# Moving every store from GpSimd's software ring to SyncE's ring, beside the loads

## The chip, the cores and the metric

The kernel runs on one core of one Trainium2 chip. The metric is device time in microseconds (us), taken over several executions; the profile is one execution, and its span is about 2 us shorter than the reported time. All timed runs below that are compared with one another were in the fast state. The four copy kernels were run once each, so their state is unknown, and only single stretches of their traces are used.

## The reference

The forward pass mixes two branches with a scalar gate: attention of one query over a cache (32 heads, 4096 keys, head size 128) and a small MLP with the mish activation. The kernel returns the output and nine gradients.

```python
def _fwd_reference(A_x, A_k_cache, A_v_cache, A_wq, A_wo, B_x, B_w1, B_b1, B_w2, gate_w):
    # ... (_A_ref: q = x @ wq; p = softmax(q k^T / sqrt(128)); o = p v; return o @ wo)
    # ... (_B_ref: h = x @ w1 + b1; return (h * tanh(softplus(h))) @ w2)
    x = A_x
    g = _sigmoid((x * gate_w).sum(-1, keepdims=True))
    a = _A_ref(x, A_k_cache, A_v_cache, A_wq, A_wo)
    b = _B_ref(x, B_w1, B_b1, B_w2)
    return g * a + (1 - g) * b

def reference(A_x, A_k_cache, ..., grad_out):     # arguments cut
    _out, _vjp = jax.vjp(_f, A_x, A_k_cache, A_v_cache, A_wq, A_wo, B_w1, B_b1, B_w2, gate_w)
    return (jnp.asarray(_out), *[jnp.asarray(_g) for _g in _vjp(grad_out)])
```

What matters for the time: K and V are 32 MB each, and so are their gradients dK and dV. With the weights and their gradients 82 MB are read and 82 MB written, all in bfloat16.

## The kernel before

Each head is one period. The loads of K and V (1 MB each) are issued three heads ahead by SyncE into four buffers each; dK of the head before is stored early in a period, dV of this head late, both by GpSimd, from a pool of five buffers. The transfers of one issuer stand in line in its ring: the page lists SyncE's as q1 (hardware) and GpSimd's as q0 (software). Sixteen DMA engines carry each transfer in packets, and each engine leaves a landing mark when its part is done. The tile of `wo` is overwritten in place by its gradient, stored, and its buffer loaded anew.

```python
    def load_k(h):
        if h < H:
            kts[h] = kv_in.tile([P, J, Dh], BF16, name="Kn", tag="Kn", bufs=KB)
            nc.sync.dma_start(kts[h][:], Kv[h])
    # ... (load_v, load_wq, load_w2 and w1 are alike)
    def load_wo(g):
        if g < NG:
            wos[g] = wts.tile([P, G, D], BF16, name="wo_g", tag="wo_g", bufs=3)
            nc.sync.dma_start(wos[g][:], wo_v[g])
    # ...
    def dk_half(h, half):
        # ... (VectorE: outer product of ds and q, one half of the 4096 rows)
        if h == H - 1:
            a, b = half * (J // 2), (half + 1) * (J // 2)
            nc.gpsimd.dma_start(dKv[h][:, a:b, :], st["dK"][:, a:b, :])
        elif half == 1:
            nc.gpsimd.dma_start(dKv[h], st["dK"][:])
    # ... (dv_half is alike)
    for h in range(H):
        hh, g = h % G, h // G
        if hh == 3:
            load_wo(g + 2)
            # ... (load_wq every second group)
        load_k(h + 3)
        load_v(h + 3)
        # ...
        period(h)     # holds dk_half(h - 1, 0..1) early and dv_half(h, 0..1) late
    # ... (last gradients, then the small outputs)
    nc.gpsimd.dma_start(dwq_v[:, :, CL:], dwq_l[:])
```

## Time and profile before

| | before |
|---|---|
| time, median of 4 runs | 417.73 us (417.38 to 418.01) |
| span of the profile | 415.7 us |
| last store (dwq_l) landed: first / fifteenth / last of its sixteen marks | 403.2 / 404.2 / 411.4 us |
| from the last landing to the end of the span | 4.3 us |

The prediction below shows and reads the page's rows. Three further views are needed for the comparison. First the DMA issues of the page (last column: median us from issue to landing):

```profile
Kn<-in_A_k_cache_dram SPq DMA_DIRECT2D x32, 1024.0 KB, 27.0
Vn<-in_A_v_cache_dram SPq DMA_DIRECT2D x32, 1024.0 KB, 27.8
out_dram<-dV_sb POOLq DMA_DIRECT2D x32, 1024.0 KB, 12.3
out_dram<-dK_sb POOLq DMA_DIRECT2D x31, 1024.0 KB, 12.4
```

Then the wait for an output buffer, from the costliest groups (count, then busy us and mean ns of one, then idle time before and what ended it):

```profile
L557 DVE TENSOR_TENSOR dV_sb<-p_bf,qd 128x2048 bf16<-128x2048 bf16 x64 | 78.0, 1218 | 4.1 <-DMA out_dram<-dK_sb 4.1
```

Last, the closing drain of GpSimd (the instructions of the program's last line; durations in ns, min/median/max, then the first and last start in us):

```profile
L788 POOLq DRAIN  x3: 45/102/17856, 397.0 to 415.4; - x3
```

The longest of these three drains starts at 397.05 us, right behind GpSimd's last issue, and lasts 17.856 us, to 414.9. The last store had landed at 411.4. So for 3.5 us no data moves and the program waits for GpSimd alone. The prediction passed this by: it took the time after the last landing as fixed.

### The profile page before, as it was taken

The page shows a single profiled execution, that of the slowest core. Times are in us where ns is not written, and L with a number is a line of the kernel's source. Part 1 is how long each engine was busy: PE and PEld are TensorE (multiplying, and loading weights), DVE is VectorE, ACT ScalarE, POOL GpSimd, SP SyncE. Part 2 cuts the span into 40 slices and gives each one's busy share as a digit, 9 for nine tenths or more (in the row PEclk, how much of TensorE's full clock was granted, in tenths as well). Part 3 has the DMA queues.
Part 4 walks back from the last instruction along what each step waited for, and adds up shares of the span by engine and source line. Part 5 has one row for each costly group of instructions (what it writes and reads, how often), then busy time and mean ns, then how long its engine had stood idle before and what let it go on. Part 6 is the DMA issues. An engine that isn't in the chain of part 4 may idle for free.

```text
span 415.7 us, 15639 instructions
## 1 busy us (share of the span) xinstructions
PE 305.6 (74%) x6932; PEld 281.1 (68%) x6932; DVE 308.2 (74%) x804; ACT 174.4 (42%) x394; POOL 49.3 (12%) x92
## 2 busy tenths in 40 slices
PE   0787999888998788788877688429888788876200
PEld 0676888888987677787767687428777678876200
DVE  2348666665679999989897688528999997967850
ACT  1354444334445455354533346305553545553000
POOL 0001110111110111121111112001111111132310
PEclk9999999969999999989996899958999999998655
DMA  8999999999999999999999999999999999998980
GB/s 280 419 401 335 420 424 417 420 423 423 421 423 420 420 404 415 424 420 423 423 410 426 423 414 411 419 422 381 405 411 423 419 419 422 421 422 351 401 314 14
DMA packets 26336, 165.06 MB, mean 397 GB/s; under 512 B 2812, under 2 KB 2812, under 8 KB 10012
## 3 DMA queue, kind: packets, MB, share of 16 engines
q1 hardware_dynamic: 14116, 82.03, 48.6%
q0 software_dynamic: 12112, 82.03, 47.7%
q8 instruction: 54, 0.88, 0.8%
q14 instruction: 14, 0.11, 0.1%
q10 hardware_dynamic: 40, 0.01, 0.0%
HBM read 82.03 MB, written 82.03 MB: 395 GB/s over the span
## 4 chain that ended last, share of the span: by engine, by line
DMA 37%; DVE 30%; PE 21%; ACT 6%; issue 2%; ACTq 0%; DVEq 0%
DMA Kn<-in_A_k_cache_dram 30%; PE tr L535 7%; DVE dK_sb L557 7%; DVE dV_sb L557 6%; DMA out_dram<-dK_sb 6%; ACT tT L537 5%; DVE junk L354 4%; PE sA L601 3%; PE sA L543 3%; PE sB L654 3%; DVE junk L268 3%; PE h_ps L385 2%; DVE junk L486 2%; DMA vec_rows<-in_gate_w_dram 1%; DVE wo_g L343 1%
## 5 line engine op out<-in xcount | busy, mean ns | idle before, releaser
L537 ACT COPY tT<-tr 128x512 f32<-128x512 f32 x256 | 142.9, 587 | 153.1 <-PE tr L535 153.0
L543 PEld LDWEIGHTS <-tT 128*128 128x128 bf16 x2048 | 75.8, 98 | 37.0 <-ACT tT L537 31.6
L535 PE MATMUL tr<-ident_bf,Kn 128*128 128x128 bf16 x1024 | 79.2, 230 | 9.4 <-DMA Kn<-in_A_k_cache_dram 8.2
L557 DVE TENSOR_TENSOR dV_sb<-p_bf,qd 128x2048 bf16<-128x2048 bf16 x64 | 78.0, 1218 | 4.1 <-DMA out_dram<-dK_sb 4.1
L557 DVE TENSOR_TENSOR dK_sb<-ds_bf,qd 128x2048 bf16<-128x2048 bf16 x64 | 77.7, 1216 | 0.0
L535 PEld LDWEIGHTS <-Kn 128*128 128x128 bf16 x1024 | 66.2, 104 | 10.9 <-DMA Kn<-in_A_k_cache_dram 9.3
L535 PE MATMUL tr<-ident_bf,Vn 128*128 128x128 bf16 x1024 | 72.8, 221 | 0.2 <-DMA Vn<-in_A_v_cache_dram 0.2
L543 PE MATMUL sA<-qdc,tT 128*128 128x48 bf16 x1024 | 49.2, 188 | 23.0 <-ACT dq_all L659 16.3
L535 PEld LDWEIGHTS <-Vn 128*128 128x128 bf16 x1024 | 63.2, 100 | 1.4 <-issue 0.7
L543 PE MATMUL sB<-qdc,tT 128*128 128x48 bf16 x1024 | 46.3, 183 | 0.6 <-issue 0.6
L654 PE MATMUL sB<-ds_bf,Kn 128*128 128x48 bf16 x1024 | 32.6, 185 | 7.7 <-DVE ds_bf L643 4.8
L584 POOL DMA_DIRECT2D out_dram<-dV_sb x32 | 18.3, 571 | 169.1 <-DVE dV_sb L557 82.1
L601 PEld LDWEIGHTS <-Vn 128*128 128x128 bf16 x1024 | 30.3, 96 | 10.4 <-issue 10.3
L601 PE MATMUL sA<-e_bf,Vn 128*128 128x48 bf16 x1024 | 30.9, 183 | 7.4 <-DVE zs L621 5.4
L574 POOL DMA_DIRECT2D out_dram<-dK_sb x31 | 17.7, 570 | 153.1 <-DVE rz L623 84.6
L654 PEld LDWEIGHTS <-Kn 128*128 128x128 bf16 x1024 | 29.7, 97 | 8.3 <-issue 8.3
L605 DVE TENSOR_REDUCE m<-sA 128x1 f32<-128x32 f32 x32 | 6.1, 189 | 31.7 <-PE sA L543 31.5
L268 DVE SCALAR_TENSOR_TENSOR junk<-wo_g,da_bc 128x640 bf16<-128x640 bf16 x32 | 26.3, 821 | 2.9 <-DMA wo_g<-in_A_wo_dram 1.2
L354 DVE SCALAR_TENSOR_TENSOR junk<-wq_g,dq_bc 128x1024 bf16<-128x1024 bf16 (+1 forms) x25 | 25.1, 1004 | 0.2
L385 PE MATMUL h_ps<-cols_bf,w_sb 128*96 128x1 bf16 x90 | 18.3, 314 | 1.2 <-ACT qd L279 0.5
L641 DVE TENSOR_SCALAR_CACHE_REDUCE dj<-sB,rz 128x128 f32<-128x128 f32 x32 | 11.1, 345 | 10.8 <-PE sB L635 10.8
L385 PEld LDWEIGHTS <-w_sb 128*96 128x96 bf16 x90 | 17.6, 272 | 1.6 <-issue 0.6
(137 smaller groups left out, 277.5 us busy)
## 6 DMA issues: line engine op xcount, KB each, us to landing
Kn<-in_A_k_cache_dram SPq DMA_DIRECT2D x32, 1024.0 KB, 27.0
Vn<-in_A_v_cache_dram SPq DMA_DIRECT2D x32, 1024.0 KB, 27.8
out_dram<-dV_sb POOLq DMA_DIRECT2D x32, 1024.0 KB, 12.3
out_dram<-dK_sb POOLq DMA_DIRECT2D x31, 1024.0 KB, 12.4
wq_g<-in_A_wq_dram SPq DMA_DIRECT2D x4, 1280.0 KB, 21.8
wo_g<-in_A_wo_dram SPq DMA_DIRECT2D x8, 640.0 KB, 13.3
out_dram<-wo_g POOLq DMA_DIRECT2D x8, 640.0 KB, 11.3
out_dram<-dwq_t POOLq DMA_DIRECT2D x5, 896.0 KB, 16.2
```

What stands on the lines that cost most here:

```text
L268: nc.vector.scalar_tensor_tensor(junk[:, 0:D], in0=wos[g][:, i, :], scalar=1.0, in1=da_bc[:], op0=ALU.mult, op1=ALU.mult, accum_out=gp["do ...
L354: nc.vector.scalar_tensor_tensor(junk[:, c0:c1], in0=wqs[w][:, rc, c0:c1], scalar=1.0, in1=dq_bc[:, w * WG * Dh + c0:w * WG * Dh + c1], op ...
L385: nc.tensor.matmul(hps[a][:, fc:fc + 1], lhsT=w1_sb[:, rc, :].rearrange("p (q c) -> p q c", c=FCN)[:, :, fc], rhs=x_bf[:, rc:rc + 1], star ...
L535: nc.tensor.transpose(tp[:, t, :], src[:, c * 8 + t, :], ident_bf[:])
L537: nc.scalar.copy(f32v(sb[:].rearrange("p a b -> p (a b)")), f32v(tp[:].rearrange("p a b -> p (a b)")))
L543: nc.tensor.matmul(out[:, j:j + W], lhsT=tb[:, t, :], rhs=vec.to_broadcast([P, W]), start=True, stop=True)
L557: nc.vector.tensor_tensor(dst[:, a:b, :].rearrange("p j (a b) -> p j a b", b=2), col[:, a:b, :].unsqueeze(2).to_broadcast([P, n, Dh // 2, 2]),
L574: nc.gpsimd.dma_start(dKv[h], st["dK"][:])
L584: nc.gpsimd.dma_start(dVv[h], st["dV"][:])
L601: nc.tensor.matmul(O, lhsT=vts[h][:, j, :], rhs=st["e"][:, j:j + 1].to_broadcast([P, W]), start=(j == 0), stop=(j == J - 1))
L641: nc.vector.tensor_scalar(dj[:], PT, rz[:], None, ALU.mult, ALU.add, accum_out=dd[:])
L654: nc.tensor.matmul(DQ, lhsT=kts[h][:, j, :], rhs=ds[:, j, 0:1].to_broadcast([P, W]), start=(j == 0), stop=(j == J - 1))
```

## The change

All stores that GpSimd issued are issued by SyncE, in the order in which the program states them, so they stand on the same hardware ring as the loads (one small output stays on ScalarE, as before). The intent is to have one ring in the program's own order, no software ring, and a GpSimd with nothing to do. Nothing else changes; the instructions of TensorE, VectorE and ScalarE are the same.

```diff
-            nc.gpsimd.dma_start(dwo_v[g], wos[g][:])
+            nc.sync.dma_start(dwo_v[g], wos[g][:])
 ...
-            nc.gpsimd.dma_start(dKv[h], st["dK"][:])
+            nc.sync.dma_start(dKv[h], st["dK"][:])
 ...
-            nc.gpsimd.dma_start(dVv[h], st["dV"][:])
+            nc.sync.dma_start(dVv[h], st["dV"][:])
 ...
-    nc.gpsimd.dma_start(dwq_v[:, :, CL:], dwq_l[:])
+    nc.sync.dma_start(dwq_v[:, :, CL:], dwq_l[:])
 ... (the same for dw2, db1, dw1, the two halves of the last dK, and dwq)
```

> **What bounds the kernel now.** I read the row of DMA tenths first, then the queue table, then single stretches of time, then the waits of SyncE's queue, and last the marks that each transfer leaves when it lands.
>
> The page of the kernel before:
>
> ```profile
> span 415.7 us, 15639 instructions
> ...
> PE 305.6 (74%) x6932; PEld 281.1 (68%) x6932; DVE 308.2 (74%) x804; ACT 174.4 (42%) x394; POOL 49.3 (12%) x92
> ...
> DMA  8999999999999999999999999999999999998980
> GB/s 280 419 401 335 420 424 417 420 423 423 421 423 420 420 404 415 424 420 423 423 410 426 423 414 411 419 422 381 405 411 423 419 419 422 421 422 351 401 314 14
> ...
> q1 hardware_dynamic: 14116, 82.03, 48.6%
> q0 software_dynamic: 12112, 82.03, 47.7%
> q8 instruction: 54, 0.88, 0.8%
> ```
>
> No compute engine is above 74%, while the DMA digits are 9 nearly everywhere and the rate sits at 420 GB/s. The two big queues hold 48.6% + 47.7% = 96.3% of the time of 16 engines: q1 is the loads (SyncE), q0 the stores (GpSimd). So this is a copy of 82 MB in and 82 MB out with arithmetic beside it.
>
> The same in stretches (columns: window, length, busy time per engine, granted clock, DMA share, GB/s):
>
> ```profile
> 12.00:22.00 10.00, 6.49 (x96) 5.64 (x94) 3.48 (x12) 3.51 (x8) 0.00 (x0) 1.00 1.01 416
> 40.00:140.00 100.00, 88.37 (x1853) 83.16 (x1853) 67.26 (x180) 44.30 (x102) 9.58 (x18) 0.97 1.01 421
> ...
> 380.00:400.00 20.00, 7.59 (x157) 6.42 (x154) 17.66 (x48) 3.30 (x8) 5.65 (x9) 0.67 1.00 398
> ...
> 404.00:411.00 7.00, 0.00 (x0) 0.00 (x0) 0.00 (x0) 0.00 (x0) 0.00 (x0) 0.50 0.06 25
> ```
>
> Loads alone on one ring run at 416, both rings at 421, stores alone at 398, all with a DMA share of 1.0. The last line is the important one: from 404 to 411 the share is 0.06, and 0.06 x 16 engines is 1.0 engine. One DMA engine alone works for the last 7 us. The sixteen landing marks of each transfer say the same: the load of K issued at 199.77 us was landed by the first engine at 218.0, by the fifteenth at 227.1 and by the last at 234.8; the last store (dwq_l) at 403.3, 404.2 and 411.4. One engine trails the others by about 8 us, and a transfer has landed only when that one is done.
>
> Why does it trail? The packet records show the 54 instruction fetches of q8, 16 KB each, about 1.0 us apiece among other packets; a fetch fits in one engine. During the store-only tail the trail grows from 11.3 to 12.4 us behind the first engine over two fetches (375 to 389.6 us) and does not grow from 392 to 411, with one fetch at 390 and none later. So I take the trailing engine to be the one that fetches instructions, not one that suffers from the software ring.
>
> Is that engine ever idle? Between 195.2 us (landing of a K load) and 411.4 us (last store) the loads and stores that it finished sum to 87.8 MB / 16 = 5.48 MB for it. An 8 KB packet starts 306 ns after the one before, so that is 5.48 MB / 8192 B x 0.306 us = 205 us of 216 us. The remaining 11 us are 28 fetches at 0.4 us (estimate). Nothing is left over: the trailing engine is busy all the time, and so it, not the average engine, sets the end.
>
> **What the Trainium skill says.** All from the page "DMA: Bandwidth & Descriptors". (1) Section "Issuing engines are not separate DMA queues": transfers from SyncE, ScalarE and GpSimd run on the same 16 DMA engines and interleave; several issuers only save issue time. The trace agrees: 416 GB/s with one ring, 421 with two. (2) Section "Queues, rings and completion order": each DMA engine goes round-robin over the rings that have work, packet by packet, and one ring is consumed in order. The trace agrees: with both rings full a K load takes 27.0 us and a store of the same size 12.3, because the shorter ring gets half of the engine. (3) Section "Latency and other measured facts": engines 7 and 15 are usually slower, with the descriptor ring of the software path as best guess. If that were the cause of the trailing engine, this change would cure it; the store-only tail, where only the software ring works and the trail stays at 7 to 8 us behind the fifteenth, speaks against.
>
> **The change part by part.**
>
> Removed: 85 or so GpSimd issues (0.53 us each, 49.3 us busy in all with the start). GpSimd is 12% busy and on no part of the chain of waits that I print, so this is worth 0 us, except that a store starts perhaps 0.3 us earlier (dV done at 234.24, issue at 234.54).
>
> Added: as many issues on SyncE, 0.33 us each when nothing blocks, 28 us in 415. SyncE is idle otherwise: 0 us.
>
> Moved: 82 MB from q0 to q1. Work of each DMA engine is unchanged: 10.3 MB of data at 306 ns per 8 KB, about 385 us, plus 54 x 0.4 = 22 us of fetches on the trailing engine, 407 us. It starts at about 1.5 us and ends at 411, so at most 2 to 3 us of idle time are there to win.
>
> Latency: loads and stores now stand in one line. A transfer waits for everything issued before it, about 7 to 8 MB, so 17 to 20 us: loads fall from 27 to about 19 us, stores rise from 12 to about 19. K is loaded three heads ahead (2.5 periods of 12.2 us = 30 us before its use), the five output buffers return after 2.5 periods as well. Both are longer than 20 us, so compute should not be held up more than it is by the DMA rate itself.
>
> Order on SyncE: the waits now come in program order. A store waits for VectorE; the next loads wait for the product that reads K last, which comes after that same work of VectorE. So a store's wait ends before the wait of the load behind it nearly always. The exception is the reload of wo:
>
> ```profile
> SPq L117 <- PE sB L654: 167.1, 20, 16.0
> SPq L132 <- DMA out_dram<-wo_g: 60.4, 5, 18.1
> ```
>
> The first line is the ordinary wait for a free K buffer. The second is SyncE standing still five times, 12 us each, until the store of the updated wo has landed. That store is issued one period (12 us) before the reload. With 20 us in place of 11 it lands later, so SyncE stands there perhaps 6 to 9 us longer, five times. But behind that store one head of loads and two output stores are already in the ring, 4 MB or 10 us of work, so the DMA engines go on. On the path to the end: 0 to 1 us each, at most 3 us in all.
>
> Reads and writes in phases: with one line all engines read 2 MB, then write 2 MB. Stores alone ran at 398 against 421 GB/s; part of that is their smaller rows, and for the trailing engine I get about 3% from its landings in the tail (16.0 MB in 40.2 us, less 1.2 us for three fetches: 410). If all 82 MB were written in pure phases it would be 3% of 195 us = 6 us; the engines drift apart by up to 10 us, which mixes the phases again, so I take a third to a half: +2 to +3 us.
>
> Sum: -1 (earlier issue, less idle) + 1 (wo waits) + 2 (phases) = +2 us on 417.7: **419.5 us**.
>
> **The rivals.**
>
> Rival A, head-of-line blocking: a store whose data is late, or the wo reload, blocks loads long enough to empty the ring. For it: 60.4 us of such waits exist already, and after the one of 18.1 us compute stood still later (the chain of waits has a K load of 33.66 us at 245.38). Against it: even then the DMA row shows 411 to 422 in those slices, and 381 in one. If each of five reloads emptied the ring for 3 us, +15 us: 433.
>
> Rival B, the trailing engine is slow because of the software ring. Then it catches up with the others, which end at 403.5: -8 us, and some more as the others no longer wait: 400 to 409. Against it stands the tail, where the trail does not grow between fetches.
>
> Rival C, one ring is less efficient than two (a bubble at each completion). Against it: loads alone on q1 from 12 to 22 us ran at 416 with share 1.01, and stores alone on q0 landed 2.2 to 2.5 us apart per 0.9 to 1.0 MB with no gap. A bubble of 0.1 us on 165 transfers would be +16 us; nothing of the kind is visible.
>
> **Range and chances.** The floor is the trailing engine's 407 us + 1.5 at the start + 4.7 after the last landing = 413, plus 2 us between span and reported time (415.7 against 417.7): 415, with some 3 us of uncertainty in the fetches. So I set the low end at 412.5. The high end is phases in full (+6) and half of rival A's stalls (+5): 428. Faster by over 2% (below 409.4) needs rival B: 0.05. Slower by over 2% (above 426.1) needs A or C: 0.17. The rest, 0.78, is within 2%.
>
> **What would show it.** q0 disappears and q1 carries 164 MB at a share near 96%. K loads land in about 19 us, stores of dK and dV in about 19. The wait of the wo reload on its store rises from 60 to 90 us or more. The GB/s row stays between 410 and 424 from the fifth slice to the thirty-sixth; lower by 1 to 2% than before if phases matter. In the last 7 us before the final landing one engine still works alone (share 0.06): if that is gone, rival B was right. If slices show a DMA share under 0.9 beside a SyncE wait on wo or on VectorE, rival A was right. If the share stays at 1.0 with the rate below 410, it is C or the phases.

## The result, and the profile after

The changed kernel took 421.89 us (median of 4 runs, 420.47 to 422.35), against 417.73. The ratio is 1.0094 (95% interval 1.0068 to 1.0121). Here and below a ratio is the mean time of one kernel's fast runs over that of the other's fast runs of the same rounds, so it isn't quite the ratio of the medians quoted. The verdict is "within 2%", slower by about 1%, and the interval excludes equality.

The page after:

```profile
span 419.7 us, 15633 instructions
...
PE 308.5 (74%) x6932; PEld 283.4 (68%) x6932; DVE 308.6 (74%) x804; ACT 174.7 (42%) x394; POOL 0.8 (0%) x8
...
DMA  8999999999999999999999999999999999998990
GB/s 285 418 395 271 420 419 410 418 419 424 418 422 418 421 417 411 422 419 414 404 389 404 422 383 356 420 419 412 397 381 422 421 420 423 415 419 369 406 384 23
...
q1 hardware_dynamic: 27108, 164.06, 96.6%
```

The software ring is gone and one ring carries everything; GpSimd fell from 49.3 us busy to 0.8. The DMA digits are as full as before. The rate row is new in its second half: 404, 389, 383, 356, 397, 381 where the kernel before had 410 to 426 in most slices.

The issues after:

```profile
Kn<-in_A_k_cache_dram SPq DMA_DIRECT2D x32, 1024.0 KB, 18.2
Vn<-in_A_v_cache_dram SPq DMA_DIRECT2D x32, 1024.0 KB, 19.9
out_dram<-dV_sb SPq DMA_DIRECT2D x32, 1024.0 KB, 19.3
out_dram<-dK_sb SPq DMA_DIRECT2D x31, 1024.0 KB, 19.1
```

Loads and stores now take the same 18 to 20 us, as one line of transfers must. In this program SyncE stops once eight transfers are under way: the dK store issued at 216.31 us follows the landing at 216.25 of the transfer issued eight before it, and the next two issues, at 219.35 and 222.08, follow landings at 219.28 and 222.02. Eight transfers at 2.5 us each are the 20 us. Before, each ring had its own eight.

SyncE's queue waits after, and the wait for an output buffer:

```profile
SPq L132 <- DMA out_dram<-wo_g: 31.1, 5, 9.4
```

```profile
L557 DVE TENSOR_TENSOR dV_sb<-p_bf,qd 128x2048 bf16<-128x2048 bf16 x64 | 78.0, 1219 | 30.0 <-DMA out_dram<-dK_sb 28.0
```

The wait for the reload of wo fell from 60.4 to 31.1 us. VectorE's wait for a free output buffer rose from 4.1 to 28.0 us, because a store takes longer to land. Neither seems to set the end (the first is tested below, the second is only argued), as the stretches suggest (length, busy time per engine, granted clock, DMA share, GB/s):

```profile
12.00:22.00 10.00, 6.62 (x97) 5.65 (x95) 3.33 (x12) 3.72 (x8) 0.00 (x0) 1.00 1.01 417
40.00:140.00 100.00, 88.48 (x1852) 83.50 (x1852) 67.04 (x179) 44.57 (x101) 0.00 (x0) 0.97 1.01 419
...
411.00:418.00 7.00, 0.00 (x0) 0.00 (x0) 0.00 (x0) 0.00 (x0) 0.00 (x0) 0.50 0.07 26
```

The last 7 us before the final landing look as they did: 0.07 of sixteen engines, one engine alone. So the end is still set by the DMA engine that trails, and the question is what that engine lost. I read it from the sixteen landing marks that each transfer leaves in the trace. A 1 MB transfer gives each engine eight packets of 8 KB, and at 306.5 ns each that is 2.46 us (other sizes with the packet durations seen in quiet stretches). Call the elapsed time, less the work that the last marks prove done (a transfer under way is counted in proportion), the engine's **lost time**; it is an estimate, and it contains the start, the fetches and every slow packet:

```
lost time of the trailing engine, us, by time t
t (us)     40    100    180    300    390   | last landing   span
before    8.5   10.1   14.6   20.4   25.4   |   411.4       415.7
after    10.3   12.1   16.4   25.7   31.7   |   418.3       419.7
```

The changed kernel loses 1.8 us more in the first 40 us, nothing more from 40 to 180, and 4.5 us more from 180 to 390 (15.3 against 10.8). With a few tenths after that it is the 6.9 us by which the last landing moved. Yet the span grew by only 4.0, since the closing drain is gone:

```profile
L788 POOLq DRAIN  x3: 34/78/469, 1.0 to 419.5; - x3
```

From the last landing to the end are now 1.4 us instead of 4.3, which gives back 2.9. In all: +6.9 - 2.9 = +4.0 us.

The 6.9 us aren't spread evenly. In two short passages the loads of w2 (720 KB each) land. From 28 to 40 us, before and after:

```profile
28.00:40.00 12.00, 9.28 (x244) 8.63 (x242) 9.91 (x24) 5.93 (x14) 1.73 (x3) 1.00 1.02 333
28.00:40.00 12.00, 8.85 (x229) 8.20 (x226) 9.70 (x25) 5.72 (x14) 0.00 (x0) 0.99 1.02 273
```

From 205 to 230 us, before and after:

```profile
205.00:230.00 25.00, 19.17 (x420) 17.45 (x416) 21.48 (x52) 10.97 (x25) 2.20 (x5) 0.86 1.02 421
205.00:230.00 25.00, 16.64 (x367) 15.10 (x368) 19.09 (x46) 9.68 (x22) 0.00 (x0) 0.93 1.01 397
```

The DMA share is as full, yet less is moved. Here most engines are slower and not only the one that trails: from 205 to 230 us the packet records of the changed kernel have 87 packets of 7.5 to 8 KB that lasted over 0.42 us (14 before), up to fourteen of them side by side (three before). The kernels below agree: from 205 to 230 us late_sync and swap_first, with two rings, ran at 418 GB/s, and wo_pool, all_pool_first and alternate, with one, at 392, 402 and 395. In these 25 us the trailing engine lost 1.7 to 2.0 us on two rings and 3.1 to 4.4 on one (estimates from the marks, as above). So about 2 of the 4.5 us fall into them, and the 1.8 us of the first 40 arise mostly in the first passage. Why loads of w2 cost more on one ring was not tested.

Where do the slow packets lie? With one ring the transfers land in their order, so consecutive last marks time each of them. Between 120 and 375 us the trailing engine's 52 stores took 0.28 us more than the quiet packets would, its 48 loads 0.09 us: 14.5 + 4.3 = 18.8 us, beside 19.6 us lost between 100 and 390. The store of dK issued at 216.31 took it 2.80 us; the load of K issued at 210.98 took 2.47. In the last 20 us, with the arithmetic over, stores took 2.46 to 2.50 us again. So on one ring the packets of K and V lose mainly in stores, on this engine, while the compute engines work.

Is that new? The packet records allow a comparison. On one engine a packet starts 3 or 4 ns before the one before it ends (more than nine in ten of the links that I followed), so the trailing engine's packets can be chained back from its last marks. From 275 to 398 us of the changed kernel the chain has no gap: the engine never ran dry. An 8 KB store packet took 332 ns from start to start there, a load packet 311. In the kernel before, from 240 to 394 us, they took 315 to 320 and 325 to 330. The sum of a pair is nearly the same, 642 against 640 to 650 ns: on two rings the slowness is shared out to the loads, not gone. So slow stores on this engine by themselves don't tell the two kernels apart.

### The profile page after: what moved, and what is told of

The parts are those of the page before. It is cut to its first block, busy times and chain, and to the rows that moved or that the text cites. A ratio compares the mean times of both kernels' runs of the same rounds, so it can differ in the third digit from the quotient of the medians.

```text
span 419.7 us, 15633 instructions
## 1 busy us (share of the span) xinstructions
PE 308.5 (74%) x6932; PEld 283.4 (68%) x6932; DVE 308.6 (74%) x804; ACT 174.7 (42%) x394; POOL 0.8 (0%) x8
## 4 chain that ended last, share of the span: by engine, by line
DMA 33%; DVE 26%; PE 26%; ACT 8%; issue 3%; ACTq 0%; DVEq 0%; SPq 0%
DMA out_dram<-dK_sb 28%; PE tr L535 9%; DVE dV_sb L557 7%; ACT tT L537 7%; DVE dK_sb L557 5%; DMA Kn<-in_A_k_cache_dram 4%; PE sB L654 4%; PE sA L601 3%; PE sA L543 3%; PE h_ps L385 3%; DVE junk L354 3%; DVE junk L268 3%; DMA vec_rows<-in_gate_w_dram 1%; DVE dj L641 1%; DVE ds_bf L643 1%
## 5 line engine op out<-in xcount | busy, mean ns | idle before, releaser
L535 PE MATMUL tr<-ident_bf,Kn 128*128 128x128 bf16 x1024 | 77.1, 226 | 2.0 <-issue 1.4
L535 PE MATMUL tr<-ident_bf,Vn 128*128 128x128 bf16 x1024 | 75.1, 225 | 0.0
L535 PEld LDWEIGHTS <-Kn 128*128 128x128 bf16 x1024 | 65.0, 102 | 2.8 <-issue 1.7
L535 PEld LDWEIGHTS <-Vn 128*128 128x128 bf16 x1024 | 65.6, 102 | 1.0 <-issue 0.5
L543 PE MATMUL sA<-qdc,tT 128*128 128x48 bf16 x1024 | 49.3, 188 | 22.9 <-ACT dq_all L659 15.7
L654 PE MATMUL sB<-ds_bf,Kn 128*128 128x48 bf16 x1024 | 34.5, 189 | 26.0 <-DVE ds_bf L643 20.8
L654 PEld LDWEIGHTS <-Kn 128*128 128x128 bf16 x1024 | 31.9, 100 | 27.3 <-issue 27.3
L601 PEld LDWEIGHTS <-Vn 128*128 128x128 bf16 x1024 | 30.2, 95 | 11.1 <-issue 11.1
L354 DVE SCALAR_TENSOR_TENSOR junk<-wq_g,dq_bc 128x1024 bf16<-128x1024 bf16 (+1 forms) x25 | 25.1, 1004 | 0.2
L625 ACT ACTIVATE p_bf<-e_bf,rz 128x64 bf16<-128x64 bf16 x32 | 11.1, 348 | 14.0 <-DVE rz L623 12.3
L451 DVE SCALAR_TENSOR_TENSOR junk<-w2c,dm,db_bc 96x640 bf16<-96x640 bf16 x18 | 15.7, 873 | 0.2
L609 PE MATMUL sA<-ident_f,m 128*128 128x128 f32 x32 | 9.7, 303 | 7.6 <-DVE m L605 7.6
## 6 DMA issues: line engine op xcount, KB each, us to landing
Kn<-in_A_k_cache_dram SPq DMA_DIRECT2D x32, 1024.0 KB, 18.2
Vn<-in_A_v_cache_dram SPq DMA_DIRECT2D x32, 1024.0 KB, 19.9
```

What stands on the lines that cost most here:

```text
L354: nc.vector.scalar_tensor_tensor(junk[:, c0:c1], in0=wqs[w][:, rc, c0:c1], scalar=1.0, in1=dq_bc[:, w * WG * Dh + c0:w * WG * Dh + c1], op ...
L451: nc.vector.scalar_tensor_tensor(junk[0:FP, 0:D], in0=w2cs[c][:, i, :], scalar=m["dm"][:, fc:fc + 1], in1=db_bc[0:FP, :], op0=ALU.mult, op ...
L535: nc.tensor.transpose(tp[:, t, :], src[:, c * 8 + t, :], ident_bf[:])
L543: nc.tensor.matmul(out[:, j:j + W], lhsT=tb[:, t, :], rhs=vec.to_broadcast([P, W]), start=True, stop=True)
L601: nc.tensor.matmul(O, lhsT=vts[h][:, j, :], rhs=st["e"][:, j:j + 1].to_broadcast([P, W]), start=(j == 0), stop=(j == J - 1))
L609: nc.tensor.transpose(MM, m32[:].to_broadcast([P, P]), ident_f[:])
```

## The experiments

Three theories were on the table. **Ring**: with both rings full the trailing engine has packets of the other ring to go on with when a store is slow; with one ring it has not. **Phases** (the prediction's term): reading and writing in blocks costs. **Stand** (rival A): SyncE stands before the wo reload and starves the engines. The drain after the last landing came out as a fourth matter. (The expectations call the first of these Theory 1.)

| kernel | time, us (range) | ratio to before (95%) | last landing / span, us |
|---|---|---|---|
| all_pool | 428.70 (427.31 to 431.07) | 1.0270 (1.0240 to 1.0300) | |
| swap | 420.81 (420.50 to 421.15) | 1.0076 (1.0057 to 1.0094) | |
| alternate | 425.67 (424.74 to 427.58) | 1.0199 (1.0176 to 1.0223) | 422.0 / 423.4 |
| wo_pool | 421.85 (420.90 to 422.92) | 1.0098 (1.0079 to 1.0117) | 417.8 / 419.2 |
| late_sync | 415.08 (414.38 to 415.74) | 0.9938 (0.9924 to 0.9952) | 412.1 / 413.7 |
| swap_first | 414.42 (414.01 to 414.78) | 0.9924 (0.9912 to 0.9936) | 410.6 / 412.2 |
| relief15 | 431.77 (428.27 to 433.57) | 1.0337 (1.0306 to 1.0368) | |
| all_pool_first | 423.34 (422.67 to 424.17) | 1.0140 (1.0119 to 1.0162) | 418.4 / 422.2 |

The kernel before had medians of 417.40 beside the first four, 417.46 beside the next three and 417.47 beside the last. All eight gave correct results. By the 2% rule all_pool and relief15 are slower, alternate is unclear, and the others are within 2%. Lost times and landings come from one profiled execution each.

### One software ring, and the two rings with their issuers exchanged

In the first kernel every load and store of the changed kernel is issued by GpSimd; in the second, only the loads are, and SyncE issues the stores.

```diff
 all_pool, against the kernel after: each load and store
-            nc.sync.dma_start(kts[h][:], Kv[h])
+            nc.gpsimd.dma_start(kts[h][:], Kv[h])
```

```diff
 swap, against the kernel before: each load, then each store
-            nc.sync.dma_start(kts[h][:], Kv[h])
+            nc.gpsimd.dma_start(kts[h][:], Kv[h])
-            nc.gpsimd.dma_start(dKv[h], st["dK"][:])
+            nc.sync.dma_start(dKv[h], st["dK"][:])
```

> Loads and stores all on GpSimd's software ring, in the same hand order as the changed kernel: one ring again, but the software one. Theory 1 (one ring costs time because a trailing DMA engine's slow store packets can no longer lie beside load packets of another ring): about 422 us as with SyncE alone, 420 to 425. Theory 2 (the loss comes from SyncE or from the hardware ring, not from there being one): near 418, or anything far from 422.

> Loads on GpSimd's software ring, stores on SyncE's hardware ring: two rings, the roles exchanged. Theory 1 (two rings are what matters): 417 to 419 us. Theory 2 (stores on the hardware ring are themselves slower): about 422 us.

They took 428.70 and 420.81 us. Both carry a flaw of my making, which the waits of VectorE in the second show (us in total, times, longest):

```profile
DVE ident_bf L166 <- POOL a_acc L218: 18.1, 1, 18.1
```

GpSimd builds the identity matrix, and there it now did so behind its load issues: VectorE waited 18 us for it at the start. Neither time can be read against the theories. They were repeated with the identity built first.

### Reads and writes alternating

The load of V moves from ahead of the period to right behind the store of dK, so that the line alternates at 1 MB instead of 2.

```diff
         dk_half(h - 1, 1)
+        load_v(h + 3)
         e = st["e"] = small.tile([P, J], BF16, name="e_bf", tag="e_bf")
 ...
         load_k(h + 3)
-        load_v(h + 3)
```

> The changed kernel with the load of V moved behind the store of dK, so that the one ring holds load, store, load, store in place of two loads and two stores. Theory 1 in the form of phases (reads and writes of 5 us each cost, mixing them finer helps): 1 to 3 us below the changed kernel, about 420. If only the presence of a second ring counts, unchanged at 422. If order on SyncE matters (V is issued later), slower, above 423.

It took 425.67 us, slower than the change itself, and its trailing engine lost 18.4 us between 180 and 390 where the change lost 15.3. Shorter phases didn't help, so this doesn't support the phases. It is the third branch of what was expected (V issued later: above 423); what in the later place of the V load costs the further 3 us was not followed.

### The wo reload off SyncE's line

```diff
-            nc.sync.dma_start(wos[g][:], wo_v[g])
+            (nc.gpsimd if g > 2 else nc.sync).dma_start(wos[g][:], wo_v[g])
```

> The changed kernel with the reloads of wo from the fourth on issued by GpSimd, so that SyncE no longer stands still for the store of the updated wo. Rival A (these stands drain the ring and cost the time; the first engines run dry for 5 us at 251): back to 418 us. Theory 1 (the trailing DMA engine is busy all through those stands, so they cost nothing): within 1 us of 422, with the dips in the GB/s row gone.

It took 421.85 us, ratio 1.0098 against the change's 1.0094. SyncE no longer stands before wo, and the time is the same to within the intervals. Its rate row:

```profile
GB/s 285 417 399 310 419 421 410 420 420 422 418 422 418 419 418 412 421 422 411 420 361 412 421 420 405 404 399 403 421 421 425 415 414 418 393 419 290 402 381 23
```

The dips moved (361 in the twenty-first slice, none of 356 in the twenty-fifth) and the end did not. The leading engine shows the same: by 300 us it had lost 13.2 us here and 16.6 in the changed kernel, while the trailing one had lost 25.1 and 25.7. The stand starves the engines that are ahead, and they have the time. Rival A falls, as far as it is about wo.

### The last stores from SyncE

The kernel before, with only the stores of the last two heads, of dwq and of the last wo group on SyncE.

```diff
-            nc.gpsimd.dma_start(dKv[h], st["dK"][:])
+            (nc.sync if h >= H - 2 else nc.gpsimd).dma_start(dKv[h], st["dK"][:])
 ... (dV alike; dwo if g == NG - 1)
-    nc.gpsimd.dma_start(dwq_v[:, :, CL:], dwq_l[:])
+    nc.sync.dma_start(dwq_v[:, :, CL:], dwq_l[:])
```

> The kernel before with only the last stores (from the last two heads on, the dwq stores and the last dwo) moved to SyncE, when its loads are over. In the kernel before the last store lands at 411.4 and GpSimd's closing drain ends at 414.9; in the changed kernel 418.3 and 419.1. If the drain is the price of stores on GpSimd that are still in flight at the end: about 3 us less than before, 414 to 415. If the drain only waits for the landing by another way: 417.5.

It took 415.08 us, ratio 0.9938: 2.4 us less than before, at the upper edge of the 414 to 415 expected. Its last instructions:

```profile
L788 POOLq DRAIN  x3: 45/102/28982, 370.6 to 413.4; - x3
```

GpSimd's long drain begins after its last store at 370.6 us and is over at 399.6, well ahead of the end. The last landing is at 412.1, within 0.7 us of before, and the span ends 1.6 us later. So the wait on GpSimd in the kernel before, 2.4 us of its time, is shown to hang on who issues the last stores. In its two-ring part the trailing engine lost 11.5 us between 180 and 390, as before.

### Two rings exchanged, with the identity first

```diff
 swap, and ahead of the first load:
+    ident_f = const.tile([P, P], F32, name="ident_f")
+    nc.gpsimd.memset(ident_f[:], 0.0)
+    nc.gpsimd.affine_select(...)                 # arguments cut, as they stood below
     load_wq(0)
 ...
-    nc.gpsimd.memset(a_acc[:], 0.0)
+    nc.vector.memset(a_acc[:], 0.0)              # b_acc alike
```

> The exchange of roles again (loads on GpSimd, stores on SyncE), with the identity matrix built by GpSimd ahead of its loads, since in the first exchange compute waited 18 us for it. Theory 1 (two rings keep the trailing engine's losses small, whichever holds the stores) and a short closing drain: 414 to 416. If stores on the hardware ring are slower in themselves: 420 to 421 as in the first exchange.

It took 414.42 us, ratio 0.9924, and is the fastest version of the study, ahead of both kernels. Rate and queues on its page:

```profile
GB/s 222 423 410 418 417 423 414 418 424 421 420 424 420 423 398 417 423 421 422 421 415 420 423 419 417 419 426 419 380 421 425 420 421 424 417 423 346 407 378 21
...
q0 software_dynamic: 12416, 82.03, 48.6%
q1 hardware_dynamic: 13012, 82.03, 47.7%
```

It has SyncE's stores, as the change has, and the software ring, as the kernel before has. The row stays near 420, the trailing engine lost 11.3 us between 180 and 390, and the end comes 1.6 us after the last landing at 410.6. Neither the store on a hardware ring nor its issue from SyncE is what costs; one line for both is the difference left.

### Taking work off the trailing engine

If one engine is behind because it always is the same one, less data for it should bring the end forward. In every fourth head the load of K is cut so that the last eight partitions are a transfer of their own.

```diff
-            nc.sync.dma_start(kts[h][:], Kv[h])
+            if h % 4 == 2:
+                nc.sync.dma_start(kts[h][0:120], Kv[h][0:120])
+                nc.sync.dma_start(kts[h][120:128], Kv[h][120:128])
+            else:
+                nc.sync.dma_start(kts[h][:], Kv[h])
```

> The kernel before with eight of the 32 K loads cut in two: 120 partitions, then 8. If the trailing DMA engine is the last of the sixteen, it has 8 x 2.46 = 20 us less to do, no engine works alone at the end, and the next slowest sets the time: 408 to 413. If the trailing engine is another one, its load is the same or 2.5 us more: 417 to 420.

A miss: 431.77 us, 14 us slower. In its marks one engine did run ahead (a landing at 349.6 us against 357.5 for the next and 374.3 for the last), but the trail behind it stayed, so the engine relieved wasn't the trailing one. The cut transfers also cost in the rate row:

```profile
GB/s 287 417 275 368 420 423 413 386 416 422 376 381 420 418 418 403 373 422 419 410 363 398 420 414 390 406 414 371 371 378 422 406 413 403 420 422 337 389 345 14
```

Which engine trails, and whether relieving it would pay, stays open.

### One software ring, with the identity first

```diff
 swap_first, with the stores left on GpSimd as before
```

> Loads and stores all on GpSimd's ring as before, with the identity matrix built ahead of the loads so that compute starts in time. Theory 1 (one ring, whichever, lets the trailing engine lose about 5 us more than two rings, and 2 us more around the w2 loads): the last landing near 418, plus GpSimd's 3 us closing drain: 422 to 426. If the ring's kind were what counts (hardware ring bad, software ring good): 418.

It took 423.34 us, ratio 1.0140. The trailing engine lost 14.5 us between 180 and 390, in the range of the one hardware ring and not in that of two rings. The last landing is at 418.4, as in the changed kernel (418.3). The end is later by what GpSimd's drain adds:

```profile
L788 POOLq DRAIN  x3: 51/101/17366, 404.1 to 421.9; - x3
```

It lasts from 404.05 to 421.42. So in the lost time it is the number of rings that counts, not their kind. All kernels whose marks I followed, side by side:

```
lost time of the trailing engine, us     at 40   180 to 390
two rings   before                        8.5      10.8
            late_sync                     8.6      11.5
            swap_first                    8.2      11.3
one ring    after                        10.3      15.3
            wo_pool (stores all on one)  10.1      16.1
            all_pool_first               10.8      14.5
            alternate                    10.4      18.4
```

### Copies without and with work on TensorE

To see whether one ring costs by itself, four kernels only load every K and V and store the same tile as dK and dV; the weights are copied at the end, one after the other, so the total isn't compared. Their results are wrong on purpose. copy_one has all on SyncE, copy_two its stores on GpSimd; copy_one_pe adds 112 matmuls of 128x128 by 128x128 per head that read K's tile; copy_one_tiny adds the same number of tiny ones.

```diff
 copy_two, against copy_one
-            nc.sync.dma_start(v[h], tiles.pop((nm, h))[:])
+            nc.gpsimd.dma_start(v[h], tiles.pop((nm, h))[:])
```

```diff
 copy_one_pe, against copy_one; in copy_one_tiny the operands are ident_bf[0:32, 0:32] and kt[0:32, j, 0:1]
+        for k in range(7):
+            ps = gr_ps.tile([P, 4, P], F32, name="spin", tag="gr")
+            for j in range(16):
+                nc.tensor.matmul(ps[:, j % 4, :], lhsT=ident_bf[:], rhs=kt[:, j, :], start=True, stop=True)
```

> Only the transfers, no arithmetic (wrong results on purpose): every K and V loaded and stored back from the same buffer, all on SyncE. If the slow store packets of the trailing engine come from the transfers themselves: they show here too, one engine trails by several us at the end, some 405 us. If they come from compute running beside the stores: all engines end within 2 us of each other, 393 to 400 us.

> The same transfers with stores on GpSimd. If one ring is less efficient than two in itself: 5 us or more below copy_one. If it is so only where an engine is slowed: within 3 us of copy_one.

> copy_one with 112 matrix products per head on TensorE that read the K tile (their results are not used), so that instructions are fetched and SBUF is read. If fetches or TensorE's reading slow one engine: a trail of several us as in the whole kernel and a time some 5 us or more above copy_one. If neither: as copy_one.

> copy_one_pe with every matrix product cut from 128x128 by 128x128 to 32x32 by 32x1: as many TensorE instructions and as many fetches of them, one sixteenth or less of the reading of SBUF. If TensorE's reading of SBUF is what slows the stores of one DMA engine: the trail when the last V is stored is near the 2 us of copy_one. If it is the fetching or counting of instructions: near the 13 us of copy_one_pe.

The stretch from 100 to 290 us in copy_one and in copy_two (busy time of the engines that work at all, clock, DMA share, GB/s; in copy_two the second count is GpSimd):

```profile
100.00:290.00 190.00, 0.00 (x0) 0.00 (x0) 1.00 1.01 426
```

```profile
100.00:290.00 190.00, 0.00 (x0) 20.71 (x39) 1.00 1.01 427
```

426 and 427 GB/s: one ring alone is no worse than two. The same stretch in copy_one_pe (TensorE first, then its weight loads) and in copy_one_tiny:

```profile
100.00:290.00 190.00, 131.81 (x2099) 128.56 (x2097) 0.00 (x0) 0.00 (x0) 0.93 1.01 424
```

```profile
100.00:290.00 190.00, 59.69 (x2128) 58.07 (x2128) 0.00 (x0) 0.00 (x0) 1.00 1.01 424
```

The mean hardly moves; the trail does:

```
                  fetches   last V store   first to    fifteenth   trailing engine, us per MB
                            landed at      last mark   to last     store    load
copy_one             0        320.8          2.0         0.1       2.451    2.477
copy_two             0        321.8          1.8         0.0         -        -
copy_one_tiny       28        327.3          9.7         2.2       2.542    2.502
copy_one_pe         28        331.1         13.3         5.5       2.632    2.498
```

All four totals are single runs (438.57, 412.61, 443.89 and 448.10 us for copy_one, copy_two, copy_one_tiny and copy_one_pe, with the weights' slow part in them). By its total copy_two meets the branch "5 us or more below copy_one", but the 26 us lie in the weights: from the last V store to the end of the span it is 116.0 us in copy_one and 89.0 in copy_two. With TensorE at work the copy shows what the whole kernel shows: stores slow on the trailing engine, loads nearly untouched. Tiny matmuls, which share with the large ones their number of instructions and the 28 instruction fetches, bring 7.7 of the 11.3 us of spread. The other 3.6 go with larger matmuls, which read more of SBUF and last longer; these two were not separated. A copy with two rings and matmuls was not run, so that two rings shield anything while TensorE works is shown by the whole kernels alone.

## Why the prediction was right or wrong

The time came out 2.4 us above the 419.5 predicted, inside the range and on the side foretold. By its steps:

- **The bound** held. One engine works alone at the end in both kernels, and wo_pool shows that SyncE's stand before wo was free.
- **Latency** held: 19 us were predicted for loads and stores alike, 18.2 to 19.9 were measured.
- **The wo wait** went the other way: 31.1 us instead of 90 or more. SyncE reaches that point later, because it already waits for earlier landings. Its price, put at 0 to 1 us each and +1 in the sum, was 0 in wo_pool.
- **Compute not held up more** was wrong as a statement of waits (4.1 to 28.0 us for the output buffers); I found no sign of it in the end, as the trailing engine worked on without a gap. The rate row was to stay between 410 and 424 (the kernel before had not stayed there either: 381 to 426) and fell to 356, as the engines that are ahead ran dry.
- **The phases, +2 to +3 us**, are the step that failed. The sign was right, the mechanism was not supported: copies in 2 MB blocks on one ring ran at 426 GB/s against 427 on two, and alternating in smaller blocks was slower. In its place stands what the trailing engine lost more on one ring: 6.9 us at the last landing, of which 1.8 in the first 40 us and about 2 between 205 and 230 us, both around loads of w2 where most engines were slow, and the rest over the remaining time. Whether those passages are phases of another kind was not tested.
- **Less idle, -1 us**, was not seen: the trailing engine lost more, not less.
- **4.7 us after the last landing** were taken as fixed. They were 4.3, and 3.5 of them were GpSimd's drain; the change took out 2.9. This missing gain hid two fifths of the loss. That the two errors partly cancelled is luck, and why the sum of +2 stood so near the measured +4.2.
- **The trailing engine as the one that fetches, at 0.4 us a fetch**, is not borne out. A fetch lasted 0.88 to 1.22 us in the packet records, and of the 49 fetches in the stretches of the changed kernel in which this engine's packets could be chained (40 to 215, 222 to 267 and 275 to 398 us) one lies on it, at 79.5 us; of the 28 in copy_one_pe and in copy_one_tiny one each. In the tail of the kernel before, from which the prediction read the fetches, a fetch of 1.02 us began at 379.0, but none of this engine's transfers that landed from 377 to 392 us took over 0.30 us too long: the trail grew there through slow stores. What does bring the trail is work on TensorE: without it the fifteenth mark and the last were 0.1 us apart, with it 2.2 and 5.5. The stated mechanism doesn't hold, and I have no full one. Open are why one engine, why its stores, and why mostly from about 120 us on.
- **Rival B** falls: without any software ring the last mark is still 8.4 us behind the fifteenth (418.3 against 409.9), 7.2 before. **Rival A** falls with wo_pool for the reload of wo; for stores whose data is late only the chain without a gap speaks against it. **Rival C** as stated, a loss of one ring in itself, falls with the copies of K and V; that one ring loses while the compute engines work is what came in its place.

What is shown: one ring instead of two moves the last landing from 410.6 to 412.1 us to 417.8 to 422.0 in this kernel, whichever ring it is, and SyncE as issuer of the last stores saves 2.4 us. What is not shown is why. The **Ring** theory, that on two rings a slow store is covered by the other ring's packets, finds little support in the chained packets, where a store and a load together take as long on two rings as on one. One ring also means eight transfers under way in place of sixteen; the two were not separated, though the chain without a gap speaks against an engine that ran dry.

## What to carry to other kernels

When copies bound a kernel, look at each transfer's last landing mark and not at the mean rate: a drop from 420 to 356 GB/s cost nothing where it fell on engines that were ahead, while one from 421 to 397 that fell on most of them, the one behind too, went with about 2 us of loss. If the trace shows an engine that trails, try loads and stores on two rings, and let an engine without a long closing drain issue the last stores. And read what lies between the last landing and the end of the span before calling it fixed.

## What the Trainium skill lacked or had wrong

- "DMA: Bandwidth & Descriptors", section "Issuing engines are not separate DMA queues": it says that several issuers save only the time of issuing. Here the last store landed at 410.6 to 412.1 us with two rings, whoever issued what (before, late_sync, swap_first), and at 417.8 to 422.0 with one (after, wo_pool, all_pool_first, alternate); the trailing engine lost 10.8 to 11.5 us on two rings and 14.5 to 18.4 on one between 180 and 390 us. In copies without arithmetic the sentence held (426 and 427 GB/s).
- The same page, section "Latency and other measured facts": its guess for the slower engines is the software path's descriptor ring, and it calls the effect specific to that path. Here one engine was 8.4 us behind the fifteenth with no software ring in use, and in a hardware-ring copy the distance was 0.1 us without TensorE and 5.5 with it. Which engine it was, the trace doesn't say.
- "VectorE: DVE Perf Modes", section "The DRAIN you can't avoid", tells two kinds of DRAIN apart, the pipeline flush and a constant one of about 12 ns. It lacks a third: GpSimd's closing drain behind its stores lasted 17.86 us and ended 3.5 us after their last landing (414.9 against 411.4), and SyncE's lasted 7 ns. No page that I found has it.
